# The first expert's blocks written out part by part on every engine, with the bounds check moved to the second expert

## The chip, the cores and the metric

The kernel runs on one core of one Trainium2 chip. A core has TensorE (PE, matrix products, with a queue of its own for loading weights), VectorE (DVE), ScalarE (ACT), GpSimd (POOL) and SyncE (SP, which only issues transfers here). Each engine runs its instructions in its own order; one that waits for a semaphore holds up all behind it on that engine. 16 DMA engines move data between HBM and SBUF. Products go to eight PSUM banks of 128 x 512 float32; the kernel uses five of them under the tag `big` and three under `att`.

The metric is the device time of one execution in microseconds. A run's time is a median of several executions.

## The reference

A linear attention with a decaying state, then two feed-forward layers ("experts"), all in float32. Four batches, eight heads of 48, 768 steps; 3072 tokens of width 384 in the two layers.

```python
# r, k, v: (4, 8, 768, 48), 0.1 * randn;  w the same shape, 0.8 to 0.95;  u: (8, 48)
state = zeros(B, H, D, D)
for t in range(S):
    kt, vt, rt, wt = k[:, :, t], v[:, :, t], r[:, :, t], w[:, :, t]
    cur = einsum('bhd,bhe->bhde', u[None] * kt, vt)
    y[:, :, t] = einsum('bhd,bhde->bhe', rt, state + cur)
    state = wt[..., None] * state + einsum('bhd,bhe->bhde', kt, vt)
x = y.transpose(0, 2, 1, 3).reshape(3072, 384)

a = x @ w1; b = x @ w2          # 384 -> 1024 each
x = ((a * b) @ w3) @ w_out      # 1024 -> 1024 -> 384
h = x @ w_in                    # 384 -> 2048
out = (h - tanh(h)) @ w_out2    # 2048 -> 384
```

The first layer's w1, w2, w3, w_out and the second layer's w_in, w_out arrive in float64.

## The kernel before

**Attention in chunks.** The 768 steps of a batch are six chunks of 128, 24 chunks (n) in all. `prep(n)` loads five tiles (P, ws: the decays twice; k, r, v), checks that the decays lie within bounds (two ScalarE passes, L210 and L211, into `over`), and forms the running product of the decays (a scan on VectorE, L214), its inverse from the end of each block of 8 (L217 on GpSimd, L218, and the scan L221 on VectorE) and the decayed k and r (L238, L239; on VectorE for the first four chunks, on GpSimd later). `att(n)` forms the scores (`psA`, L259, copied by L263 and masked on GpSimd, L265), turns k (`psk`, L278), updates the state (`psu`, L285) and adds up the outputs (`psy`, L301 and L307). The diagonal, r u k, is made by small matmuls and a product (L243, L295, L313) for n < 5, and by GpSimd products, a reduction and a predicated copy (L235 to L237, L270) later. The last two heads of a chunk go to a tile `y` and are spread by six small transfers per block (L326) to the rows of `xt` that the other heads leave free.

**Weights.** Each float64 weight block is loaded as pairs of 32-bit words (`st`, three buffers) and made float32 by two ScalarE passes (L142, L145) and two VectorE passes (L146, L148). Weights and activations are kept as a rounded part and a rest (`fp32r`, two halves), and `three` (L166 to L168) forms each product of 512 columns by three matmuls.

**The first expert** works on six blocks of 512 tokens (four chunks each). For each of eight slices f of the 1024 columns, `phase1` forms a and b (18 matmuls; `psa`, `psb`), ScalarE copies a (L375), VectorE multiplies (L376), and ScalarE and VectorE split the product into `g` (L362, L363). `phase2` multiplies g by W = w3 w_out (9 matmuls into three banks `acc`). W is not loaded: `fold(f)` makes it, slice by slice, from w3 and w_out (8 products of 384 columns in float32, `psW`, L340) during the first block and the beginning of the second. phase2 follows phase1 two or three slices later. `store` writes the block to HBM (`x2d`).

**The second expert** works on the same six blocks in sixteen slices (`phase3`, `psh`), with three ScalarE squares and three VectorE products per slice in place of the tanh, and w45 as weights. `decide` gathers the checks (bounds of the decays, sizes of the weights and of x) into one flag; if it is set, a slow general path runs at the end. It does not run on these inputs.

**Order.** Program order is that of the loops from L503 on: chunk 0 to 3 and three conversions, then in block 0 and 1 lists of further parts hung on the slices (`extra`, `before`). From this a scheduler with a model of the engines sets the order on each engine; it may move any instruction past others that it does not depend on.

Of the kernel before, what the change touches and what calls it, by code (L numbers as in the profile page):

```python
# [10 lines left out]
F32 = mybir.dt.float32  # L11
# [22 lines left out]
LAG = 3  # L34
SLOTS = 14
GB = 2
GP = LAG + 2
XL = 4
ATT = 0, 1, 2, 5
ATT0 = 2, 3, 5, 6  # L40
PED = 5
KD = 4

# [31 lines left out]
def body(ctx: ExitStack, tc, rT, kT, wP, wS, vN, rN, kN, vT, uB, uN, uP, w12, w3F, wo, w45, out):  # L75
# [21 lines left out]
    ends = [const.tile([128, NP, C // SB, SB], F32, name=f"ends{i}") for i in range(2)]  # L97
    for t in ends:
        nc.gpsimd.memset(t, 0.0)
# [27 lines left out]

    def words(src, n, dst=None, clamp=False):
# [4 lines left out]
        hw = st[:, :, 1]  # L133
        m = cvp.tile([128, n], I32, tag="cm", name="cm")

        if clamp:
            nc.scalar.activation(out=m.bitcast(F32), in_=hw.bitcast(F32), func=AF.Abs, scale=2.0**-112)
            nc.vector.tensor_scalar(out=m.bitcast(F32), in0=m.bitcast(F32), scalar1=TOP, scalar2=None, op0=ALU.min)
        else:
            i = len(used)  # L140
            used.append(i)
            nc.scalar.activation(out=m.bitcast(F32), in_=hw.bitcast(F32), func=AF.Abs, scale=2.0**-112, accum_out=tops[:, i : i + 1])  # L142

        l = cvp.tile([128, n], I32, tag="cl", name="cl", bufs=2)
        nc.scalar.activation(out=l, in_=fl(st).bitcast(U8)[:, 3::8], func=AF.Identity, scale=1 / 32, bias=qa[:, 5:6])  # L145
        nc.vector.scalar_tensor_tensor(out=m, in0=m, scalar=3, in1=l, op0=ALU.logical_shift_left, op1=ALU.bitwise_or)  # L146
        to = m if dst is None else dst.bitcast(I32)
        nc.vector.scalar_tensor_tensor(out=to, in0=hw, scalar=SIGN, in1=m, op0=ALU.bitwise_and, op1=ALU.bitwise_or)  # L148
        return to.bitcast(F32)
# [6 lines left out]
    def halves_of(src, name, vec=True, clamp=False):  # L156

        t = wtile(name)
        x = words(src, 2 * DM, clamp=clamp)
        nc.scalar.copy(t[:, 0, :], x)  # L160
        (nc.vector if vec else nc.gpsimd).tensor_sub(t[:, 1, :], x, t[:, 0, :].bitcast(F32))
        return t
# [24 lines left out]

    def xtile(blk):
# [6 lines left out]
    def prep(n):  # L195
        r_d = a2.tile([128, NP, C], F32, tag="rd", name="rd")
        k_d = a2.tile([128, NP, C], F32, tag="kd", name="kd")
        P = a2.tile([128, NP, C + 1], F32, tag="P", name="P")
        w_s = a2.tile([128, NP, C], F32, tag="ws", name="ws")
        v_n = a2.tile([128, H, 64], F32, tag="vn", name="vn")  # L200
        nc.sync.dma_start(P, wP[n])
        nc.sync.dma_start(w_s, wS[n])
        nc.sync.dma_start(k_d, kT[n])
        nc.sync.dma_start(r_d, rT[n])
        nc.sync.dma_start(v_n, vN[n])
        if n == 0:
            nc.sync.dma_start(fl(ub), uB)
# [7 lines left out]
        e = ends[n % 2]  # L215
        R = a1.tile([128, NP, C // SB], F32, tag="R", name="R")
        nc.gpsimd.tensor_scalar(out=R, in0=P[:, :, SB::SB], scalar1=3e38, scalar2=1e-25, op0=ALU.min, op1=ALU.max)  # L217
        nc.vector.reciprocal(e[:, :, :, SB - 1], R)  # L218
        sx = fl(w_s)
        back = e.rearrange("p a j s -> p (a j s)")[:, ::-1]  # L220
# [3 lines left out]
        cd = a2.tile([128, H], F32, tag="cd", name="cd")  # L224
        if n < PED:
            rk = a1.tile([128, NP, C], F32, tag="rk", name="rk")
            by.tensor_mul(rk, r_d, k_d)
        else:
            r_n = a1.tile([128, DM], F32, tag="rk", name="rn")
            k_n = a1.tile([128, DM], F32, tag="vc", name="kn")  # L230
            if n == PED:
                nc.sync.dma_start(un, uN.to_broadcast([128, DM]))
            nc.sync.dma_start(r_n, rN[n])
            nc.sync.dma_start(k_n, kN[n])
            nc.gpsimd.tensor_mul(r_n, r_n, un)  # L235
            nc.gpsimd.tensor_mul(r_n, r_n, k_n)
            nc.vector.tensor_reduce(out=cd, in_=r_n.rearrange("p (h d) -> p h d", d=D), op=ALU.add, axis=AX.X)  # L237
        by.tensor_mul(fl(k_d), fl(k_d), sx)  # L238
        by.tensor_mul(r_d, r_d, P[:, :, 0:C])  # L239
        if n < PED:  # L240
            pd = attp.tile([128, NP, 2], F32, tag="att", name="psd")
            for p in range(NP):
                nc.tensor.matmul(pd[:, p, :], rk[:, p, :], ub[:, p, :], start=True, stop=True)  # L243
# [476 lines left out]
```

## Time and profile before

| | |
|---|---|
| median of 3 runs | 955.73 us (954.77 to 956.27) |
| the profiled execution | 952.14 us, its span 950.4 us |
| TensorE busy | 876.2 us (92% of the span), mean granted clock 0.966 of full |
| VectorE, ScalarE, GpSimd busy | 623.2, 490.7, 223.7 us (66, 52, 24%) |
| stores of the first expert's blocks 3 and 4 | begin at 435.78 and 501.52 us |
| stores of the second expert's block 0, then each 65 us | 625.87, 691.14, 756.42 us |

The span is from the first to the last instruction. Busy shares are means over stages with different limits, so stretches of time say more than these. The granted clock is that of TensorE, as a share of 2.4 GHz; 0.5 is the lower level, 1.2 GHz. Matmuls overlap: a single one shows 0.39 us though the next starts 0.23 us after it.

### The profile page before, as it was taken

The numbers are of one execution on the slowest core, as the hardware profiler recorded it, in microseconds if no ns is written. First come the engines' busy times: TensorE is split into PE (matmuls) and PEld (weight loads), VectorE is DVE, ScalarE is ACT, GpSimd is POOL, SyncE is SP. The second block draws the span as 40 slices with busy tenths as digits, with TensorE's granted clock in tenths as the row PEclk, the third lists the DMA queues.
The fourth block names the chain that finished last, engine by engine and source line by source line (L and its number), as shares of the span: only waits on it lengthen the run. The fifth ranks groups of instructions, "written<-read, shape, count | busy, mean of one in ns | idle before, by whom it ended". The sixth has DMA issues, their size and how long they took to land.

```text
span 950.4 us, 12862 instructions
## 1 busy us (share of the span) xinstructions
PE 876.2 (92%) x4762; PEld 700.4 (74%) x4762; DVE 623.2 (66%) x885; ACT 490.7 (52%) x880; POOL 223.7 (24%) x217
## 2 busy tenths in 40 slices
PE   3556988889999999999999999999999999999996
PEld 3445765566877777777777778888888888888885
DVE  7970755657747557647457797676676666676763
ACT  5851444345433334333247676666666666666662
POOL 3231334332534434334224530010010010100000
PEclk9656999989999999999999999999999999999999
DMA  8853254455633343342034310010020110200001
GB/s 300 279 190 95 80 182 158 136 169 205 203 92 104 94 140 128 113 108 92 31 83 155 112 56 11 1 67 1 1 67 0 37 32 1 67 1 0 34 1 37
DMA packets 38951, 87.02 MB, mean 92 GB/s; under 512 B 4832, under 2 KB 9824, under 8 KB 38880
## 3 DMA queue, kind: packets, MB, share of 16 engines
q1 hardware_dynamic: 37152, 83.76, 26.6%
q10 hardware_dynamic: 1728, 2.36, 1.3%
q8 instruction: 39, 0.64, 0.3%
q14 instruction: 32, 0.26, 0.1%
HBM read 74.31 MB, written 9.44 MB: 88 GB/s over the span
## 4 chain that ended last, share of the span: by engine, by line
PE 61%; DMA 10%; DVE 9%; issue 8%; POOL 5%; ACT 4%; SPq 0%; POOLq 0%; ACTq 0%; DVEq 0%
PE acc L168 9%; PE acc L166 8%; PE acc L167 8%; PE psh L166 7%; PE psh L167 7%; PE psh L168 7%; DMA st<-w 3%; DMA st<-w3F 2%; DMA rn<-rN 2%; PE psb L166 2%; PE psa L166 2%; PE psA L259 2%; PE psb L167 1%; PE psy L307 1%; DVE A L270 1%
## 5 line engine op out<-in xcount | busy, mean ns | idle before, releaser
L363 DVE TENSOR_TENSOR g<-psh,g 128x512 fp32r<-128x512 f32 (+1 forms) x99 | 66.6, 674 | 61.2 <-ACT g L362 61.0
L166 PE MATMUL psh<-xt,w 128*128 128x512 f32 x252 | 98.1, 389 | 1.0 <-DVE g L363 1.0
L362 ACT CAST g<-psh 128x512 fp32r<-128x512 f32 (+1 forms) x99 | 56.7, 574 | 81.7 <-DVE psh L422 81.7
L167 PE MATMUL psh<-xt,w 128*128 128x512 f32 x252 | 98.0, 389 | 0.0
L166 PE MATMUL acc<-g,w 128*128 128x512 f32 x252 | 98.0, 389 | 0.0
L168 PE MATMUL psh<-xt,w 128*128 128x512 f32 x252 | 98.0, 389 | 0.0
L167 PE MATMUL acc<-g,w 128*128 128x512 f32 x252 | 98.0, 389 | 0.0
L168 PE MATMUL acc<-g,w 128*128 128x512 f32 x252 | 98.0, 389 | 0.0
L420 DVE TENSOR_TENSOR psh<-psh,z 128x512 f32<-128x512 f32 (+1 forms) x99 | 67.3, 680 | 28.1 <-ACT z L417 28.0
L359 POOL TENSOR_TENSOR xt<-x2l,xt 128x512 fp32r<-128x512 f32 x18 | 24.5, 1375 | 252.6 <-ACT xt L358 252.5
L417 ACT ACTIVATE z<-psh 128x512 f32<-128x512 f32 (+1 forms) x99 | 58.0, 586 | 41.4 <-PE psh L168 39.8
L362 ACT CAST g<-psb 128x512 fp32r<-128x512 f32 x48 | 28.1, 585 | 97.2 <-DVE psb L376 84.5
L146 DVE SCALAR_TENSOR_TENSOR cm<-cm,cl 128x768 int32<-128x768 int32 (+1 forms) x44 | 44.9, 1021 | 45.2 <-ACT cl L145 37.7
L422 DVE SCALAR_TENSOR_TENSOR psh<-s,psh 128x512 f32<-128x512 f32 (+1 forms) x99 | 67.2, 679 | 10.2 <-DVE psh L421 0.9
L421 DVE SCALAR_TENSOR_TENSOR psh<-s,psh 128x512 f32<-128x512 f32 (+1 forms) x99 | 67.1, 678 | 8.5
L418 ACT ACTIVATE s<-z,qa 128x512 f32<-128x512 f32 (+1 forms) x99 | 70.6, 713 | 3.0
L166 PE MATMUL psa<-xt,w 128*128 128x512 f32 x144 | 59.8, 415 | 12.9 <-DMA xt<-y 11.3
L419 ACT ACTIVATE s<-z,qa 128x512 f32<-128x512 f32 (+1 forms) x99 | 68.9, 696 | 0.0
L142 ACT ACTIVATE cm<-st 128x768 f32<-128x768 f32 (+1 forms) x44 | 36.2, 823 | 51.5 <-DMA st<-w3F 34.7
L166 PE MATMUL psb<-xt,w 128*128 128x512 f32 x144 | 59.2, 411 | 3.0 <-ACT a L375 2.5
L168 PE MATMUL acc<-g,W 128*128 128x512 f32 x144 | 54.3, 393 | 3.9 <-DVE W L363 3.9
L166 PE MATMUL acc<-g,W 128*128 128x512 f32 x144 | 56.6, 393 | 1.1 <-ACT W L362 1.1
(132 smaller groups left out, 2017.9 us busy)
## 6 DMA issues: line engine op xcount, KB each, us to landing
st<-w SPq DMA_DIRECT2D x24, 768.0 KB, 4.4
st<-w3F SPq DMA_DIRECT2D x16, 512.0 KB, 4.5
P<-wP SPq DMA_DIRECT2D x24, 258.0 KB, 3.0
ws<-wS SPq DMA_DIRECT2D x24, 256.0 KB, 2.7
kd<-kT SPq DMA_DIRECT2D x24, 256.0 KB, 3.1
rd<-rT SPq DMA_DIRECT2D x24, 256.0 KB, 3.9
vn<-vN SPq DMA_DIRECT2D x24, 256.0 KB, 3.6
x2d<-o SPq DMA_DIRECT2D x18, 256.0 KB, 2.2
```

The source lines that it names most:

```text
L146: nc.vector.scalar_tensor_tensor(out=m, in0=m, scalar=3, in1=l, op0=ALU.logical_shift_left, op1=ALU.bitwise_or)
L166: nc.tensor.matmul(ps, lhs(0), rhs(1), start=start, stop=False)
L167: nc.tensor.matmul(ps, lhs(0), rhs(0), start=False, stop=False)
L168: nc.tensor.matmul(ps, lhs(1), rhs(0), start=False, stop=stop)
L362: nc.scalar.copy(t[:, 0, :], x)
L363: nc.vector.tensor_sub(t[:, 1, :], x, t[:, 0, :].bitcast(F32))
L417: nc.scalar.activation(out=z, in_=p, func=AF.Square)
L418: nc.scalar.activation(out=s1, in_=z, func=AF.Square, scale=QS, bias=qa[:, 0:1])
L419: nc.scalar.activation(out=s2, in_=z, func=AF.Square, scale=QS, bias=qa[:, 1:2])
L420: nc.vector.tensor_mul(p, p, z)
L421: nc.vector.scalar_tensor_tensor(out=p, in0=s1, scalar=QB1, in1=p, op0=ALU.add, op1=ALU.mult)
L422: nc.vector.scalar_tensor_tensor(out=p, in0=s2, scalar=QB2, in1=p, op0=ALU.add, op1=ALU.mult)
```

## The change

The first five blocks of the first expert are no longer ordered by the scheduler.

*Block 0 and the first eight chunks* are split into parts that each use one engine (`running`, `scores`, `mask`, `w_scaled`, `s_round` and so on), and a table `ORDER` of some 400 words, read from left to right, says which part of which chunk, weight block or slice comes next. A word is a short name and a number: `Sa3` the scores of chunk 3, `lwa3`, `waa3`, `wba3`, `wja3`, `wha3`, `wsa3` the load, the two ScalarE passes, the VectorE passes, the rounding and the rest of block 3 of w1 and w2 (`a`; `o` is w_out, `x` and `y` the halves of w3), `P3` and `Q3` phase1 and phase2 of slice 3, `F3` fold 3. All of chunks 0 to 7 and all eight folds come before the end of block 0.

*Blocks 1 to 4* follow a function `pair`: one chunk of the next block and two slices of this one, in a fixed order.

*The first four chunks' last two heads* are not sent through transfers: their outputs come first in `psy`, are copied (`last_out`), and three matmuls with a tile of ones and zeros (`last_place`) add them to the free rows of the same bank. For later blocks the six transfers are issued by SyncE, not ScalarE.

*The bounds check* reads the decays again during the second expert's blocks 1 to 4 (six chunks each, `bounds`), and `decide` runs in block 5 instead of block 1. The diagonal by small matmuls is used for n < 4 (was 5), the two `ends` tiles are one, and w3 has four buffers (were three). Block 5 of the first expert and the second expert are still ordered by the scheduler.

```diff
-PED = 5
+PED = 4
+ORDER = """
+LP0 LK0 lwa3 lwa1 lwa2 Da0 LP1 Dr0 K0 Db0 LK1 Dk0 Sd0 Dc0 waa3 wba3 Sa0 Se0 wja3 waa1 Sf0 wba1 St0 lwy3 Sb0 wja1 Sk0
...
+""".split()
-        d2 = ev.tile([128, NP, C], F32, tag="a", name="d2")
-        nc.scalar.activation(out=d2, in_=P[:, :, 1:], func=AF.Square, bias=qa[:, 2:3])
-        nc.scalar.activation(out=d2, in_=d2, func=AF.Relu, bias=qa[:, 4:5], accum_out=over[:, n : n + 1])
...
+        order = (KT, *range(KT)) if blk == 0 else range(NP)
+        for p in order if c else ():
...
+    def last_out(n):
+        nc.scalar.copy(last2()[1], preps[n]["py"][:, KT, :])
+
+    def last_place(n):
+        sel, y = last2()
+        for j in range(KT):
+            nc.tensor.matmul(preps[n]["py"][:, j, :], sel[:, j, :], y, start=False, stop=True, skip_group_check=True)
...
+    w3_tile = lambda: cvp.tile([128, NF // 2, 128], F32, tag="w3", name="w3", bufs=4)
...
+    with tc.manual_schedule():
+        nc.sync.dma_start(fl(ub), uB)
+        for x in ORDER:
+            k = x.rstrip("0123456789")
+            parts[k](int(x[len(k) :]))
+        store(acc0, lambda e: x2d[0, :, e, :], 0)
...
+    def pair(blk, i, acc, weights):
+        n = (blk + 1) * per + i
...
+        f = 2 * i
+        if now:
+            scores(n)
+            scores_out(n, 0)
+            mask(n, 0)
+            scores_out(n, 1)
+            mask(n, 1)
+            turn = n % NC < NC - 1
+            if turn:
+                turned(n)
+                turned_out(n)
+        pa, pb = phase1(xtile(blk), f)
+        a = gate_a(pa)
+        if nn:
+            load2(n + 2, "ws")
+            load2(n + 2, "k")
+        if now:
+            put_diag(n)
+        nc.vector.tensor_mul(pb, pb, a)
+        g = gp.tile([128, 2, TB], F32R, tag="g", name="g")
+        split_ps(pb, g)
+        if weights and i == 3:
+            conv2_halves(blk - 2)
+            largest(blk - 2)
+        if now and turn:
+            update(n)
+            state(n)
+            state_decay(n)
+        done(f, g)
+        if nn:
+            load2(n + 2, "P")
+        if nx:
+            running(n + 1)
+            block_ends(n + 1)
+            backward(n + 1)
+            decayed(n + 1)
+            ruk(n + 1)
+        if now:
+            outputs(n)
+        if weights and i == 1:
+            conv2_fetch()
+        f += 1
+        pa, pb = phase1(xtile(blk), f)
+        if now:
+            for part in (last_round, last_rest, x_round, x_rest):
+                part(n)
+            if i == per - 1:
+                spread(blk + 1, nc.sync)
+        if nn:
+            load2(n + 2, "r")
+            load2(n + 2, "v")
+        if nx:
+            ruk_sum(n + 1)
+        if nn:
+            load_n(n + 2, "kn")
+            load_n(n + 2, "rn")
+        a = gate_a(pa)
+        nc.vector.tensor_mul(pb, pb, a)
+        g = gp.tile([128, 2, TB], F32R, tag="g", name="g")
+        split_ps(pb, g)
+        if weights and i == 2:
+            conv2_act(blk - 2)
+            conv2_join(blk - 2)
+        done(f, g)
+
+    for blk in range(1, NB - 1):
+        acc = []
+        with tc.manual_schedule():
+            for i in range(per):
+                pair(blk, i, acc, blk in (2, 3))
...
+    def bounds(n):
+        w = ev.tile([128, NP, C], F32, tag="a", name="wb")
+        nc.sync.dma_start(w, wP[n][:, :, 1:])
+        nc.scalar.activation(out=w, in_=w, func=AF.Square, bias=qa[:, 2:3])
+        nc.scalar.activation(out=w, in_=w, func=AF.Relu, bias=qa[:, 4:5], accum_out=over[:, n : n + 1])
...
-        if blk == 1:
-            extra[2].append(decide)
+        if 0 < blk < NB - 1:
+            for j in range(6):
+                extra[2 * j + 2].append(lambda n=6 * blk - 6 + j: bounds(n))
+        if blk == NB - 1:
+            extra[2].append(decide)
```

How the instructions stand on an engine, before and now, at three places.

The first place is ScalarE around the copies of chunk 3's scores (`A<-psA`). `cm` and `cl` are the two passes of a weight conversion (128x768 a block of w1 and w2 or w_out, 128x512 a half of w3), `xt` and `y` the outputs of chunk 2 and then 3, `ks` the turned k. Before:

```order
L142 ACTIVATE cm,tops<-st 128x768
L145 ACTIVATE cl<-st,qa 128x768
L142 ACTIVATE cm,tops<-st 128x512
L145 ACTIVATE cl<-st,qa 128x512
L320 CAST xt<-psy 128x3x128
L320 CAST y_246<-psy 128x128
L145 ACTIVATE cl<-st,qa 128x512
L263 COPY A<-psA 128x512 x2
L280 COPY ks<-psk 128x512
```

Now:

```order
L168 ACTIVATE cm,tops<-st 128x768
L312 COPY cd<-psd 128x8
L430 CAST xt<-psy 128x3x128
L332 COPY A<-psA 128x512 x2
L174 ACTIVATE cl<-st,qa 128x768
L354 COPY ks<-psk 128x512
L168 ACTIVATE cm,tops<-st 128x768
L409 COPY y_148<-psy 128x128
```

The copies stood behind two whole conversions and the second pass of another half of w3 (128x512). Now they follow chunk 2's outputs directly, with one pass of a conversion of w_out ahead of those and the other behind the copies.

The second place is TensorE where block 1's first product (`psa<-xt` with block 0 of the weights) begins; `psW` is a fold, `acc` the second layer's product, `psA` and `psk` scores and turned k of chunk 8. Before:

```order
L301 MATMUL psy<-rd,Sb_120 64x128 x8
L307 MATMUL psy<-A,vn 64x128 x8
L340 MATMUL psW<-wo,w_1106 128x384 x4
L340 MATMUL psW<-wo,w_1107 128x384 x4
L259 MATMUL psA<-rd,kd 128x128 x8
L278 MATMUL psk<-ident,kd 128x128 x4
L166 MATMUL psa<-xt,w_0_182 128x512
L167 MATMUL psa<-xt,w_0_182 128x512
```

Now:

```order
L327 MATMUL psA<-rd,kd 128x128 x2
L486 MATMUL psW<-wo,w_1166 128x384 x4
L486 MATMUL psW<-wo,w_1362 128x384 x4
L327 MATMUL psA<-rd,kd 128x128
L486 MATMUL psW<-wo,w_1366 128x384 x4
L486 MATMUL psW<-wo,w_1248 128x384 x4
L327 MATMUL psA<-rd,kd 128x128 x2
L206 MATMUL acc<-g,W 128x512
...
L208 MATMUL acc<-g,W 128x512
L327 MATMUL psA<-rd,kd 128x128 x3
L349 MATMUL psk<-ident,kd 128x128 x4
L206 MATMUL psa<-xt,w_0_442 128x512
```

Chunk 7's outputs (`psy`) stood one fold, the scores and the turned k ahead of block 1's first product. Now they stand further up, and two folds and the second layer's products stand between.

The third place is VectorE during one pair of slices of blocks 1 to 4; `psb<-psb,a` is the gate product, `g` its rest, `P` and `ws` the two scans of the next chunk, `A<-eye,cd` the diagonal, `cd<-rn` the reduction that feeds the next chunk's diagonal. Before:

```order
L214 SCALAR_TENSOR_TENSOR P<-P,e_86 128x516
L218 RECIPROCAL ends_89<-R 128x64
L221 SCALAR_TENSOR_TENSOR ws<-ws,ends_89 128x512
L376 TENSOR_TENSOR psb<-psb,a 128x512
L270 COPY_PREDICATED A<-eye,cd 128x512
L363 TENSOR_TENSOR g<-psb,g 128x512
L270 COPY_PREDICATED A<-eye,cd 128x512
L237 TENSOR_REDUCE cd<-rn 128x8
L291 TENSOR_TENSOR Sb_119<-psu,Sb_120 128x4x48
L321 TENSOR_TENSOR xt<-psy,xt 128x3x128
L321 TENSOR_TENSOR y_2186<-psy,y_2186 128x128
L376 TENSOR_TENSOR psb<-psb,a 128x512
```

Now:

```order
L343 COPY_PREDICATED A<-eye,cd 128x512 x2
L804 TENSOR_TENSOR psb<-psb,a 128x512
L516 TENSOR_TENSOR g<-psb,g 128x512
L370 TENSOR_TENSOR Sb_117<-psu,Sb_118 128x4x48
L261 SCALAR_TENSOR_TENSOR P<-P,e_86 128x516
L289 RECIPROCAL ends<-R 128x64
L292 SCALAR_TENSOR_TENSOR ws<-ws,ends 128x512
L426 TENSOR_TENSOR y_2203<-psy,y_2203 128x128
L434 TENSOR_TENSOR xt<-psy,xt 128x3x128
L285 TENSOR_REDUCE cd<-rn 128x8
L843 TENSOR_TENSOR psb<-psb,a 128x512
L516 TENSOR_TENSOR g<-psb,g 128x512
```

The reduction, which waits for two products on GpSimd, stood behind the diagonals and between two gate products that are far apart; now it stands just ahead of each pair's second gate product, and the two scans stand between the pair's two gate products.

## Rows read from the trace of the kernel before

**Rows 1.** Stretches of the span: start:end, length, then by engine busy us (instructions), granted clock, DMA.

```profile
10.00:60.00 50.00, 29.49 (x222) 25.89 (x224) 47.36 (x59) 35.99 (x69) 15.22 (x13) 0.73 0.78 274
30.00:60.00 30.00, 17.06 (x127) 14.78 (x128) 28.36 (x38) 21.49 (x42) 8.90 (x8) 0.56 0.73 242
60.00:90.00 30.00, 15.35 (x141) 13.25 (x138) 7.12 (x10) 8.24 (x18) 7.41 (x8) 0.61 0.46 139
90.00:200.00 110.00, 94.57 (x549) 67.92 (x548) 64.62 (x86) 45.96 (x97) 38.68 (x38) 0.96 0.42 133
200.00:240.00 40.00, 39.65 (x242) 27.20 (x240) 25.31 (x34) 18.16 (x34) 15.18 (x15) 1.00 0.55 198
240.00:280.00 40.00, 40.00 (x248) 31.77 (x245) 25.86 (x35) 15.51 (x30) 17.04 (x16) 1.00 0.45 145
560.00:950.40 390.40, 382.61 (x1689) 316.19 (x1687) 266.70 (x408) 242.36 (x403) 21.05 (x16) 1.00 0.08 25
```

**Rows 2.** Chain of waits at the front: start us, us, what.

```profile
0.82 2.75 DMA P<-wP
...
4.93 0.73 ACT d L210
...
5.68 1.25 DVE P L214
```

**Rows 3.** The same chain further on.

```profile
69.65 3.87 DMA st<-w3F
...
74.26 1.05 ACT A L263 x2
...
187.38 6.54 DMA xt<-y
```

**Rows 4.** TensorE's timeline: start, length, operation, idle before and its releaser.

```profile
37.56 1.97 PE L301 MATMUL psy<-rd,Sb 48*64 48x128 f32 x16
...
88.03 0.77 PE L166 MATMUL psa<-xt,w 128*128 128x512 f32 x1 [5.30 <-DMA xt<-y]
...
91.38 0.39 PE L168 MATMUL psa<-xt,w 128*128 128x512 f32 x1
...
105.66 0.39 PE L168 MATMUL psb<-xt,w 128*128 128x512 f32 x1
```

**Rows 5.** Chain of waits: one fold, and one chunk's TensorE work at full clock.

```profile
202.37 5.36 PE psW L340 x16
...
239.08 1.09 PE psA L259 x16
...
240.17 0.59 PE psk L278 x4
...
246.45 0.60 PE psu L285 x16
...
247.06 1.02 PE psy L301 x16
...
248.08 1.02 PE psy L307 x16
```

**Rows 6.** VectorE's timeline: the product rk twice.

```profile
7.80 0.63 DVE L227 TENSOR_TENSOR rk<-rd,kd 128x512 f32<-128x512 f32 x1
...
11.80 1.47 DVE L227 TENSOR_TENSOR rk<-rd,kd 128x512 f32<-128x512 f32 x1
```

**Rows 7.** GpSimd's timeline beside it.

```profile
10.64 2.08 POOL L295 TENSOR_TENSOR vc<-vn,cd 128x512 f32<-128x512 f32 x1 [3.34 <-ACT cd L244]
```

**Rows 8.** SyncE's timeline: the stores of the first expert's blocks 3 and 4.

```profile
435.78 3.36 SPq L397 DMA_DIRECT2D x2d<-o  x3
...
501.52 4.12 SPq L397 DMA_DIRECT2D x2d<-o  x3
```

**Rows 9.** Groups of ScalarE instructions, 0 to 200 us: count, busy us, mean ns, idle before.

```profile
L210 ACT ACTIVATE d<-P,qa 128x512 f32<-128x512 f32 x10 | 7.1, 721 | 3.1 <-DMA P<-wP 3.0
L211 ACT ACTIVATE d<-d,qa 128x512 f32<-128x512 f32 x9 | 6.5, 721 | 0.2
```

More of the change, by code (lines that the diff above doesn't have):

```diff
@@ L256, in att, with diag_out, diag_v, scores @@
+    def diag_out(n):
+        nc.scalar.copy(preps[n]["cd"], fl(preps[n]["pd"]))
+    def diag_v(n):
+        t = preps[n]
+        t["vc"] = a1.tile([128, H, 64], F32, tag="vc", name="vc")
+        nc.gpsimd.tensor_mul(t["vc"], t["v"], t["cd"].unsqueeze(2).to_broadcast([128, H, 64]))
+    def scores(n):
+        t = preps[n]
+        r_d, k_d = t["r"], t["k"]
+        t["pss"] = [attp.tile([128, NP, C], F32, tag="att", name="psA") for _ in range(2)]
+        t["A"] = [None] * 2
         for p in range(NP):
@@ L293, in att, with scores_out @@
[L293 to L298 removed]
+                nc.tensor.matmul(t["pss"][q][:, p, :], k_d[o : o + D, p, :], r_d[o : o + D, p, :], start=True, stop=True)
+    def scores_out(n, q):
+        t = preps[n]
+        t["A"][q] = a2.tile([128, NP, C], F32, tag=f"A{q}", name="A")
+        nc.scalar.copy(t["A"][q], t["pss"][q])
@@ new lines, in turned_out, with update, state @@
+    def turned_out(n):
+        t = preps[n]
+        t["ks"] = a2.tile([128, NP, 128], F32, tag="ks", name="ks", bufs=1)
+        nc.scalar.copy(t["ks"], t["pk"])
+    def update(n):
+        t = preps[n]
+        t["pu"] = attp.tile([128, NP, D], F32, tag="att", name="psu")
+        for h in range(H):
+            p, q = divmod(h, 2)
+            o = 64 * q
+            nc.tensor.matmul(t["pu"][o : o + 64, p, :], t["ks"][:, p, o : o + 64], t["v"][:, h, :D], start=True, stop=True)
+    def state(n):
+        t = preps[n]
+        dst = Sb[(n + 1) % 2][:, :, :D]
+        if n % NC == 0:
+            nc.vector.tensor_mul(dst, t["pu"], t["P"][:, :, C : C + 1].to_broadcast([128, NP, D]))
+        else:
+            nc.vector.tensor_add(dst, t["pu"], Sb[n % 2][:, :, :D])
@@ new lines, in x_rest, with spread, prep @@
+    def x_rest(n):
+        py, x, _ = place(n)
+        nc.vector.tensor_sub(x[:, 1], py[:, :KT, :], x[:, 0].bitcast(F32))
+    def spread(blk, queue):
+        xt, y3 = xtile(blk), y3tile(blk)
+        for q in range(2):
+            for j in range(KT):
+                a, b = 64 * q + 16 * j, 64 * q + D
+                queue.dma_start(xt[b : b + 16, :, j, :].bitcast(F32), y3[a : a + 16].bitcast(F32))
+    def prep(n):
+        load(n, 0)
+        load(n, 1)
+        running(n)
+        block_ends(n)
+        load_rk(n)
+        ruk(n)
+        ruk_sum(n)
+        backward(n)
+        decayed(n)
@@ L329, in body, with att @@
+    def att(n):
+        if n not in preps:
+            prep(n)
+        scores(n)
+        for q in range(2):
+            scores_out(n, q)
+            mask(n, q)
+        put_diag(n)
+        if n % NC < NC - 1:
+            for part in (turned, turned_out, update, state, state_decay):
+                part(n)
+        for part in (outputs, last_round, last_rest, x_round, x_rest):
+            part(n)
+        if (n + 1) * C % TB == 0:
+            spread(n * C // TB, nc.scalar)
     w12t, Wt, w45t = [None] * NF, [None] * NF, [None] * NF2
+    w3_half = lambda f, i: (w3F[f][:, i * 512 : (i + 1) * 512], 512)
@@ L639, in body @@
         wot.clear()
[L640 to L642 removed]
+        for m in range(NF // 2):
+            words(wo[m], 2 * DM, wo_half(m), True)
+        wpair.clear()
         for f in range(NF):
```

460 lines of the change are left out of this document (270 added, 190 removed).

## The prediction

> **What bounds the kernel now.** I read the table of stretches first [rows 1]. Look along its PE column: later TensorE is busy 98 to 100% of the time (40.00 of 40 us from 240 on, 382.61 of 390.4 from 560 on), so there only less TensorE work, or fewer gaps, could help. Before 200 us it is not: 15.35 of 30 us from 60 to 90, 94.57 of 110 from 90 to 200. Most of what can be gained lies in the first 200 us. In 10 to 60 us the DVE column is full (47.36 of 50), but from 60 to 90 it falls to 7.12 of 30: the engine that bounded the start has stopped, and so has everything else.
>
> The chain of waits says why. At the front, the first scan on VectorE starts at 5.68 although its data landed at 3.57: ScalarE's bounds check on the same tile stands between [rows 2]. Later, the copy of chunk 3's scores starts at 74.26 behind a conversion that waits for a w3 load issued only at 69.65 [rows 3]; ScalarE runs in order, so the attention chain waits for weights that only the later folds need. And from 187.38 on block 1's products wait through 6.54 us of small transfers into xt [rows 3]; block 0's first one starts at 88.03 after the same kind of wait, 5.30 us [rows 4].
>
> **The change, part by part.** I count to one point that both kernels pass: the first store of block 4's result, at 501.52 [rows 8]. After it the instructions are the same apart from the bounds check.
>
> *1. Up to the first product.* VectorE has 55 instructions between its first scan and the last piece of chunk 3 (rows 10 to 64 of its written order). At the mean of 10 to 60 us, 47.36/59 = 0.80 us [rows 1], that is 44 us; at the same 95% share of busy time, 47 us. With the bounds check gone the first scan can start at 3.6 [rows 2], so VectorE alone would allow the first product at 50. TensorE is the other bound. A chunk takes 1.09 + 0.59 + 0.60 + 1.02 + 1.02 = 4.3 us at 2.4 GHz [rows 5]; the diagonal's matmuls, as many as L307's, add 1.0, and 0.7 is an estimate for the eight small ones and the three that place rows: 6 us. At 1.2 GHz it is twice that: L301 took 1.97 us at 37.56 against 1.02 [rows 4, 5], and the granted clock was 0.56 and 0.61 of full speed in 30 to 90 us [rows 1]. Four chunks are then 47 us (chunk 0 has no state product), from about 8 us: 55, and with 2 us a chunk for the copy and the mask between scores and outputs 63. So the first product starts between 50 and 63. I take 60, near the slow end, because TensorE will again wait between short bursts as it did when rows 1 showed the low level. Before: 88.03.
>
> *2. From there to the end of block 0.* The TensorE work is fixed. The products of both layers are 8 x 27 = 216 matmuls at 0.2267 us (63 steps between 91.38 and 105.66 [rows 4]) = 49.0; eight folds at 5.36 [rows 5] = 42.9; chunks 4 to 7 are 4 x 4.32, less chunk 4's scores (done before), chunk 5's two state steps and chunk 6's state product (1.09 + 1.19 + 1.02) = 14.0. Sum 106 us. The waits inside: bounded below by 0.35 of 40 us (200 to 240) and above by 15.4 of 110 (90 to 200) [rows 1]. Of the 15.4, 6 were the wait for the small transfers at 187.38 [rows 3], which now have two folds and 18 matmuls, 15 us, between their issue and their use; the other 9.4 of 110, 8.5%, I keep: 9 us. Bounds 1 to 15. Block 0 ends at 60 + 106 + 9 = 175.
>
> *3. Blocks 1 to 4.* Their work does not change: 900 matmuls of the products (four blocks and block 5's first two steps) x 0.2267 = 204.0, and sixteen chunks x 4.32 less five missing steps (2 x 1.02 + 3 x 1.19) = 63.5; sum 267.5. The method checks against the two stores: 49.0 + 4 x 4.32 - 1.0 = 65.3 for a block, measured 501.52 - 435.78 = 65.7 [rows 8]; so I add 2 for four blocks, and 1.5 from the last matmul to the store. What changes is who waits. In the new order VectorE's second gate product stands behind the reduction L285, which waits for two GpSimd products, and those wait for the backward scan. Behind that gate product are the copy and the subtraction that free the PSUM bank which TensorE needs one step later. From 240 to 280 VectorE and GpSimd worked 25.86 and 17.04 of 40 us [rows 1]: beside a step pair of 16.3 us that is 10.5 and 6.9. If they never overlapped, 17.5 us, each of the 16 pairs would lose 1.2: 19 us. The other wait that comes late is the transfers into xt, now on SyncE: 6.54 us from issue to use [rows 3] with only one second-layer step (9 x 0.2267 = 2.0), the scores and the transpose (1.7) and a little scalar work in front: 2 us at each of four block ends, 8 us. I take 8; bounds 0 and 19.
>
> *4. The bounds check.* 24 x (0.72 + 0.72) = 35 us of ScalarE [rows 9] move into the second expert's blocks 1 to 4, with 24 loads of 256 KB on SyncE's queue, which also holds the outputs and the loads of x2. Behind a check that waits for its load are ScalarE's squares, and VectorE waits for these. In 560 to 950 ScalarE was busy 242.36 of 390.4 and TensorE 382.61 [rows 1]: 148 us idle on ScalarE hide it, and five products are ahead of their use. I take 0; without that cover it would be up to 35.
>
> The three-to-four buffer change of w3 and the move of the decision to block 5 I cost at nothing: they stand beside TensorE at 98%, and a wait there would show as a gap of it.
>
> *The sum.* Block 4's store at 175 + 267.5 + 2 + 1.5 + 8 = 454 against 501.5: 47.5 us earlier. The profiled execution took 952.14 (span 950.4), so 904.6 for one like it; the runs' median is 955.73, 3.6 above that execution, and the same difference gives **908 us**.
>
> **A page of the Trainium skill that speaks against it.** The product rk took 0.63 us at 7.80 and 1.47 at 11.80 [rows 6], when GpSimd's vc ran from 10.64 to 12.72 [rows 7]. The Trainium skill, SBUF — State Buffer, section "SBUF: two separate sides", says that VectorE instructions with two SBUF inputs and GpSimd instructions share one port pair, and that the one which starts second is blocked for the whole of the other. These rows agree. By that rule GpSimd's 22 instructions before the first product (13 in 10 to 60 us of the old kernel, 1.17 us each) would hold VectorE some 10 us longer (an estimate), and its bound for the first product would be 60, not 50; the forecast would stay, and the first rival below would lose its chance.
>
> **The rivals.**
> *The order runs as tightly as its sums.* TensorE gets its full clock early and VectorE bounds the start: first product at 52, 1 us of waits after it, 3 in blocks 1 to 4. Block 0 ends at 159; 21 us less: 887. For it: VectorE's 95% share in 10 to 60. Against: the granted clock of 0.56 to 0.61.
> *TensorE stays slow and the engines wait for one another.* First product at 66, 15 us of waits, 12 in blocks 1 to 4: 924. For it: the clock rows, and that a fixed order puts one late load in front of all that is behind it.
> *The order does not do what it says.* VectorE has 155 instructions up to the end of block 0, 124 us at 0.80; at its share of 10 to 200 us, 47.36 + 7.12 + 64.62 of 190 [rows 1], that is 198 us, and the last two folds (10.7) come behind its last conversions: 209, 34 more than I count: 942, and with the products behind the folds up to 956. For it: three weight buffers, one of them held long by a half of w3's block 3. Against: the idle of 60 to 90 us had one cause, which the order takes away.
> *Slower: the pairs of blocks 1 to 4 are too tight.* One mechanism: TensorE waits in each pair for the PSUM bank behind gate product, reduction, GpSimd and scan. With VectorE, GpSimd and ScalarE strictly in turn, 25.86 + 17.04 + 15.51 of 40 us [rows 1], a pair takes 23.8, not 16.3. It decides from 47.5/16 = 3.0 us a pair; at 4 us it costs 64 in place of my 8: 964. Against: each engine's own work is well under 16.3, and most of the three overlap.
>
> **How the numbers follow.** Forecast 0.57 (its own range, from the first product at 55 to 63, waits of 5 to 13, and 3 to 14 in the blocks: 894 to 921), tight 0.14, slow clock 0.17, no gain from the order 0.05, slower 0.07. About 0.2%, 2 us, is what a measurement here can tell from no change. Of the 0.05 I put 0.03 on faster and 0.02 on the same. Faster 0.57 + 0.14 + 0.17 + 0.03 = 0.91, same 0.02, slower 0.07. The range 892 to 932 holds the forecast, all but the slow edge of the slow clock, and the near part of the tight case, some 0.8.
>
> **What the new profile would show.** Right: the first psa matmul near 60; the first scan at about 3.6; no stretch before 175 in which VectorE is idle for 10 us; no wait of psa for xt<-y of more than 2 us; block 4's x2d store near 454; the last 450 us as before. Step 1 is wrong if the first product starts before 52 or after 66; step 2 if TensorE's idle between it and block 0's last matmul is over 15 us; step 3 if TensorE waits in blocks 1 to 4 sum to over 19; step 4 if a wait of TensorE or VectorE there ends on the load of w. The whole is wrong if the granted clock or a queue makes block 0 end after 200.

## The result, and the profile after

The changed kernel takes **909.48 us** (median of 4 runs, 908.82 to 910.88); the kernel before, on the same chip, 955.25 (954.17 to 956.27). The ratio is 0.9523, with a 95% interval of 0.9506 to 0.9539. The profiled execution took 908.82 us, its span 907.1, against 952.14 and 950.4.

The same stretches as in [rows 1], from the changed kernel (length, then the busy time of each engine with its count, the granted clock, the DMA share and GB/s):

```profile
10.00:60.00 50.00, 38.16 (x387) 33.01 (x386) 43.36 (x50) 29.52 (x57) 21.62 (x21) 0.83 0.70 232
30.00:60.00 30.00, 22.42 (x264) 19.55 (x260) 26.85 (x32) 14.76 (x30) 13.95 (x13) 0.82 0.70 224
60.00:90.00 30.00, 28.38 (x159) 21.79 (x160) 25.69 (x31) 16.08 (x32) 18.38 (x16) 0.94 0.73 244
90.00:200.00 110.00, 106.72 (x617) 76.34 (x616) 69.59 (x101) 42.05 (x89) 30.45 (x31) 1.00 0.46 145
560.00:907.10 347.10, 339.64 (x1499) 280.60 (x1497) 230.91 (x356) 239.02 (x424) 15.38 (x12) 1.00 0.14 41
```

The hole is gone: from 60 to 90 TensorE is busy 28.38 us, not 15.35, and VectorE 25.69, not 7.12; from 90 to 200 TensorE has 106.72 of 110. The last stretch is full in both kernels.

TensorE's first product, which answers to [rows 4], and on SyncE the stores of blocks 0 to 4, which answer to [rows 8]:

```profile
60.02 0.50 PE L206 MATMUL psa<-xt,w 128*128 128x512 f32 x1 [1.56 <-DVE xt L434]
```

```profile
175.03 2.12 SPq L557 DMA_DIRECT2D x2d<-o  x3
256.25 2.12 SPq L557 DMA_DIRECT2D x2d<-o  x3
326.18 2.12 SPq L557 DMA_DIRECT2D x2d<-o  x3
401.62 2.12 SPq L557 DMA_DIRECT2D x2d<-o  x3
460.38 0.82 SPq L557 DMA_DIRECT2D x2d<-o  x2
```

The first product came 28.0 us earlier, block 4's store 41.1 (501.52 before). From that store to the end of the span there were 448.9 us before, and 446.7 now. So 41 of the 43 us were won up to block 4's store. From block 1's store to block 4's it takes 204.1 us, which is no less than before (203.7, from 297.80 to 501.52): all of the gain lies in front of it. In that stretch TensorE has less to do than before (busy 194.8 us, not 200.8), since more was done ahead of it, and is idle longer (9.4 us, not 3.0).

What TensorE waited for, from the first product to block 0's store and from there to block 4's (us in total, times, longest):

```profile
PE acc L208 <- DVE W L202: 2.2, 1, 2.2
PE psA L327 <- POOL kd L303: 1.6, 1, 1.6
PE psa L206 <- DVE xt L434: 1.6, 1, 1.6
```

```profile
PE psA L327 <- POOL kd L303: 3.5, 2, 2.5
PE psa L206 <- DMA xt<-y: 3.3, 1, 3.3
PE psa L206 <- ACT A L332: 1.9, 1, 1.9
PE psu L362 <- ACT ks L354: 1.6, 2, 1.4
```

### The profile page after: what moved, and what is told of

It is laid out like the page before. It is cut to its first block, busy times and chain, and to the rows that moved or that the text cites. A ratio compares the mean times of both kernels' runs of the same rounds, so it can differ in the third digit from the quotient of the medians.

```text
span 907.1 us, 12892 instructions
## 1 busy us (share of the span) xinstructions
PE 861.9 (95%) x4762; PEld 690.8 (76%) x4762; DVE 614.3 (68%) x884; ACT 483.0 (53%) x879; POOL 227.3 (25%) x223
## 4 chain that ended last, share of the span: by engine, by line
PE 49%; issue 3%; POOL 2%; DVE 1%; DMA 1%; ACT 1%; SPq 0%; ACTq 0%; POOLq 0%
PE acc L206 8%; PE acc L208 8%; PE acc L207 8%; PE psh L206 7%; PE psh L208 7%; PE psh L207 7%; POOL w L202 1%; DMA st<-w 1%; PE psa L206 1%; PE psa L207 1%; PE psa L208 1%; PE psb L207 1%; PE psb L206 1%; PE psb L208 1%; PE psy L395 0%
## 5 line engine op out<-in xcount | busy, mean ns | idle before, releaser
L515 ACT CAST g<-psb 128x512 fp32r<-128x512 f32 x40 | 23.4, 585 | 84.9 <-DVE psb L843 48.8
L206 PE MATMUL psa<-xt,w 128*128 128x512 f32 x144 | 61.8, 429 | 6.9 <-DMA xt<-y 3.3
L337 POOL TENSOR_SCALAR_AFFINE_SELECT A<-A 128x512 f32<-128x512 f32 x48 | 37.6, 804 | 90.9 <-ACT A L332 90.7
L206 PE MATMUL psb<-xt,w 128*128 128x512 f32 x144 | 56.9, 395 | 2.5 <-ACT a L531 2.2
L208 PE MATMUL acc<-g,W 128*128 128x512 f32 x144 | 56.3, 391 | 2.2 <-DVE W L202 2.2
L206 PE MATMUL acc<-g,W 128*128 128x512 f32 x144 | 57.8, 401 | 0.0
L207 PE MATMUL psa<-xt,w 128*128 128x512 f32 x144 | 57.6, 400 | 0.0
```

The costliest lines, as they stand in the source:

```text
L206: nc.tensor.matmul(ps, lhs(0), rhs(1), start=start, stop=False)
L207: nc.tensor.matmul(ps, lhs(0), rhs(0), start=False, stop=False)
L208: nc.tensor.matmul(ps, lhs(1), rhs(0), start=False, stop=stop)
L337: nc.gpsimd.affine_select(out=A, in_=A, pattern=[[0, NP], [1, C]], compare_op=ALU.is_gt, fill=0.0, base=0, channel_multiplier=-1)
```

## The experiments

Each was timed in five rounds beside the kernel before on the same chip, and its ratio is to those runs. Four chips were used, so ratios compare better than microseconds do; the changed kernel's are 0.9523 above and 0.9527 below. Its second run, on the same chip as the kernels with sixteen extra matmuls, without block 5's conversions in block 3, and with both edits, is the measure unless another is named.

**The changed kernel again.** 

> The changed kernel once more, so that the next three have it on their own chip: 907 to 914, first product at 60, block 0's store at 175, block 3's interval of 75 us.

Measured: 908.49 us (907.52 to 911.75), ratio 0.9527 (0.9498 to 0.9557). First product 59.96, block 0's store 174.10, block 3's interval 75.0.

**Block 0's order left to the scheduler.**

```
-    with tc.manual_schedule():
+    with nullcontext():
         nc.sync.dma_start(fl(ub), uB)
         for x in ORDER:
```

> Block 0's parts are written in the same order, but the scheduler may place them as it likes; the rest is the changed kernel. Theory A (it is the order that is worth the time, not that the work is cut into parts): the scheduler again puts late weight loads and their conversions ahead of the attention chain, the first product with w_12 starts at 75 to 90 instead of 60.0, and the time is 925 to 945. Theory B (cutting the work into parts of one engine each, and placing the last heads by matmul, is what helps): first product at 58 to 66, time 906 to 916.

Measured: 947.84 us, ratio 0.9930 (0.9906 to 0.9953); first product 92.92, block 0's store 212.65, 37.6 us late. ScalarE's and TensorE's waits in that kernel, 45 and 40 to 93 us:

```profile
ACT cm L168 <- DMA st<-w3F: 6.4, 3, 2.9
ACT y L409 <- PE psy L401: 5.9, 1, 5.9
```

```profile
PE psu L362 <- ACT ks L354: 6.4, 2, 4.0
PE psy L414 <- ACT y L409: 5.9, 1, 5.9
```

As in [rows 3], ScalarE stands in front of conversions that wait for w3, and TensorE for the copies behind them. Theory A holds, and 948 is past its range: the same parts, without the order, keep 7 of the 46 us. This kernel has the fourth w3 buffer as well, so that buffer by itself does not end the wait for w3. How much of the 38 us is the w3 load, and how much the rest of the order, is not separated.

**The pairs' order left to the scheduler.**

```
     for blk in range(1, NB - 1):
-        with tc.manual_schedule():
+        with nullcontext():
             for i in range(per):
                 pair(blk, i, acc, blk in (2, 3))
```

> The pairs of blocks 1 to 4 are written in the same order, but the scheduler may place them; block 0 stays in its written order. Theory A (the written order of the pairs is worth nothing by itself: 204.1 us from block 1's store to block 4's against 204.3 in the kernel before): within 4 us of the changed kernel, 905 to 914. Theory B (the pairs' order gives back the four waits for the transfers into xt, and it is only hidden by the 7 us lost in block 3): 915 to 925, with waits of 5 us of psa for xt<-y at the block ends.

Measured: 916.04 us, ratio 0.9587 (0.9552 to 0.9622), 6 to 7.5 us more than the changed kernel. Neither theory fits: the time is in B's range, but psa waits for xt<-y only once, 2.9 us. Block 0's store comes at 181.51, 6.5 us late, though block 0's order was kept; from there to block 4's (468.04) it takes 286.5 us, against 285.4 and 286.8 with the order. The stores hide that work has moved: before block 0's store TensorE did fifteen more products of block 1 (81 each for psa and psb, not 75 and 72; 3.4 us), and the second stretch has that many fewer and still takes as long. So block 0 lost some 4 us behind its first product, and the pairs' order, against A, is worth some 3 to 5 us in blocks 1 to 4. In block 0 TensorE waits once for ScalarE; ScalarE's rows just before show why:

```profile
168.40 0.50 PE L206 MATMUL acc<-g,W 128*128 128x512 f32 x1 [3.95 <-ACT W L199]
```

```profile
163.00 0.98 ACT L174 ACTIVATE cl<-st,qa 128x768 int32<-128x768 uint8 x1
167.00 0.98 ACT L174 ACTIVATE cl<-st,qa 128x768 int32<-128x768 uint8 x1 [3.02 <-DMA st<-w]
167.88 0.47 ACT L199 CAST W<-psW 128x384 fp32r<-128x384 f32 x1
```

These 128x768 conversions are of the second expert's w45; the check of its size (L657), which follows each, stands there at 170.61. Eight loads of w were issued between 135 and 181 us, none in the changed kernel. With the pairs freed, the scheduler put them inside block 0, and the fold's copy stood behind one that waited for its load. A written order keeps its own instructions in sequence; it doesn't keep others out.

**The bounds check back ahead of each scan.**

```
+        d2 = ev.tile([128, NP, C], F32, tag="a", name="d2")
+        nc.scalar.activation(out=d2, in_=P[:, :, 1:], func=AF.Square, bias=qa[:, 2:3])
+        nc.scalar.activation(out=d2, in_=d2, func=AF.Relu, bias=qa[:, 4:5], accum_out=over[:, n : n + 1])
```

> The bounds check goes back ahead of each forward scan (two ScalarE instructions of 0.72 us a chunk, 24 chunks), and the second expert has none. Theory A (only the first scan feels it, 2.1 us, and the pairs hide the rest): first scan at 5.7, first product at 61 to 64, time 911 to 914. Theory B (in a fixed order ScalarE's 1.44 us stand in front of the scan of every pair): 1 us or more for each of 16 pairs on top, 922 to 935.

Measured: 918.63 us, ratio 0.9617 (0.9583 to 0.9652), 9 to 10 us more. First product 62.59, block 0's store 182.04, block 4's 469.82. Of the 7 us at block 0's store 2.6 are there at the first product and 4.4 come later in block 0; blocks 1 to 4 lose 1 to 2.4. So A is right on the pairs (B's 1 us a pair is not there), and too low on block 0. From block 4's store to the end of the span there are 447.5 us without the check in the second expert and 446.7 with it: there it is free.

**The kernel before, with only the check moved.** 

> The kernel before, with its scheduler, and only the bounds check moved to the second expert's blocks 1 to 4 and the decision to block 5. Theory A (what the kernel with the check put back lost, 9 us, is the price of ScalarE's 1.44 us a chunk in front of each scan in any order): first product some 4 us before 88, time 944 to 949. Theory B (it costs that only where the order is fixed and the start is tight; in the kernel before the stall of 60 to 90 us, which waits for a w3 load, covers it): first product at 86 to 89, time 952 to 957.

Measured: 954.84 us against 954.49, ratio 1.0002 (0.998 to 1.0023). The first scan starts at 3.65 (5.68 before), the first product at 86.80. Theory B: with its scheduler and its stall the kernel before loses nothing by the check (the chain of waits still runs through a w3 load, 4.71 us at 61.28); in the written order the check costs 9 to 10. The two parts of the change don't add.

**Block 0's last heads by transfers.**

```
-        "V": lambda n: last_out(n) if n < per else last_round(n), "W": ... last_place(n) ..., "Z": lambda n: spread(1, nc.sync)
+        "V": last_round, "W": last_rest, "Z": lambda n: spread(n // per, nc.sync)
```

> In block 0 the last two heads are again moved into xt by twelve SyncE transfers after chunk 3, in place of the three matmuls and copies of each chunk that place them. Theory A (the transfers were on the path in block 0: 5.30 us of waiting at 88.03 in the kernel before): first product 3 to 6 us later, 63 to 66, time 912 to 916. Theory B (another chain ends at the same time, so they are hidden): first product within 1 us of 60, time 908 to 911.

Measured: 918.26 us, ratio 0.9617 (0.9583 to 0.9651). TensorE:

```profile
70.73 0.77 PE L206 MATMUL psa<-xt,w 128*128 128x512 f32 x1 [11.27 <-DMA xt<-y]
```

Theory A, and more: 10.7 us at the first product, 8.7 left at block 0's store. TensorE waited 11.27 us for the six transfers (six, not the twelve of the text above); before it had been 5.30 [rows 4].

**Sixteen matmuls ahead of the first one.**

```
+        wm0 = big.tile([128, TB], F32, tag="big", name="wm0")
+        for _ in range(WARM):   # 16
+            nc.tensor.matmul(wm0[:, :128], ident, ident, start=True, stop=True)
```

> Sixteen 128x128 matmuls of the identity, whose result nobody uses, stand ahead of the first psd matmul on TensorE; the rest is the changed kernel. Theory A (TensorE at its lower level up to 34 us sets the first product): TensorE gets its full clock earlier, the first product starts at 52 to 57, the time is 902 to 906. Theory B (VectorE, with GpSimd beside it, sets it, and TensorE's clock is hidden): first product at 59 to 61, the time within 2 us of the changed kernel; if the extra matmuls delay the first psd, up to 3 us later.

Measured: 909.63 us, ratio 0.9527 (0.9496 to 0.9558); first product 61.49. TensorE's first work in the changed kernel (first run), then in this one:

```profile
8.58 1.87 PE L309 MATMUL psd<-ub,rk 128*128 128x2 f32 x8 [8.58 <-DVE rk L297]
10.38 2.08 PE L327 MATMUL psA<-rd,kd 48*128 48x128 f32 x16
...
24.14 2.50 PE L327 MATMUL psA<-rd,kd 48*128 48x128 f32 x16 [1.06 <-issue]
...
36.28 1.16 PE L327 MATMUL psA<-rd,kd 48*128 48x128 f32 x16
```

```profile
2.20 6.70 PE L750 MATMUL wm<-ident 128*128 128x128 f32 x32 [2.20 <-POOL ident masks.py:199]
9.23 1.05 PE L310 MATMUL psd<-ub,rk 128*128 128x2 f32 x8 [0.33 <-DVE rk L298]
10.56 1.16 PE L328 MATMUL psA<-rd,kd 48*128 48x128 f32 x16 [0.28 <-DVE kd L304]
```

The sixteen (counted as 32 there) brought the full clock to these two groups: the scores took 1.16 us, as they do at 36.28, and not 2.08. It did not last. The next matmuls on TensorE, psk, waited 2.53 us for ScalarE and took 1.12 (0.66 at full clock, at 37.51 in the changed kernel), and chunk 1's scores took 2.49, as without the sixteen. So nearly all of the lower level before 34 us was still there, and theory A was not tested. Nor are the 1.5 us at the first product shown to come from the clock: ScalarE's first weight conversion, ahead of the copy that psk waits for, began at 10.99 and not 9.19, when its load had landed; and with the same sixteen and one more edit (below) the first product came at 60.19. An estimate of what is left for theory A: at 36.90 VectorE had waited 2.65 us for chunk 1's outputs, and behind that it hardly waited; a full clock up to there would win 2.65 us at most by this wait.

The row of stretches must not be read for this: it gives the changed kernel a granted clock of 1.00 from 10 to 20 us, where the scores took 2.08 us.

**wo's conversions behind the end of xt.**

```
-... Db4 lwo3 wao2 wjo1 Dc4 ... T3 X3 lwa4 wjo2 wao3 U3 Sa4 LP5 wbo3 Y3 lwy0 P0 Sb4 wjo3
+... Db4 lwo3 wao2 Dc4 ... T3 X3 U3 Sa4 LP5 Y3 P0 wjo1 lwa4 wao3 wjo2 wbo3 lwy0 Sb4 wjo3
```

> In block 0's written order the conversions of wo's blocks 1 and 2 move behind the subtraction that completes xt; with them the later loads that need their buffers. The rest is the changed kernel. In its trace VectorE is idle for 0.2 us from 36.9 to 60.0, and these four instructions, at 53.96, 54.92, 57.33 and 58.54, take 5.0. Theory A (VectorE's queue sets the first product): it starts at 55 to 56.5; if nothing behind it is short of VectorE, the time is 4 to 5 us less than the changed kernel, 903 to 906; if TensorE then waits for the folds of wo instead, the gain is given back by block 0's store. Theory B (TensorE's lower level sets it): first product at 59 to 61, time 907 to 911.

Measured: 910.77 us, ratio 0.9525 (0.9499 to 0.9551); first product 59.10, 0.9 earlier for 5.0 us less on VectorE. The end of chunk 3 on TensorE in this kernel:

```profile
51.35 1.12 PE L349 MATMUL psk<-ident,kd 128*128 128x128 f32 x4 [3.40 <-DVE xt L434]
52.40 1.97 PE L389 MATMUL psy<-rd,Sb 48*64 48x128 f32 x16
...
57.00 0.94 PE L414 MATMUL psy<-y 128*128 128x128 f32 x6
57.87 1.16 PE L327 MATMUL psA<-rd,kd 48*128 48x128 f32 x16
59.10 0.50 PE L206 MATMUL psa<-xt,w 128*128 128x512 f32 x1
```

Without the two conversions VectorE waits for TensorE (2.34 and 1.05 us before L370 and L434), and the first product follows straight on chunk 4's scores. The numbers are theory B's. The rows say more than B: TensorE's chain ends last, but it waited 3.40 us for VectorE on the way, and its lower level here (psy in 1.97 us, not 1.09) came behind that wait. The two engines' chains end within 1 us of each other.

**All of wo's conversions there.** 

> The same with all of wo's conversions, on ScalarE too: block 0's 2.6 us at 45.90 and block 3's besides, and the later loads that need their buffers come later still. Theory A: first product at 52 to 54; the conversions that are put off then meet the gates and the chunks 4 and 5 on VectorE, which was busy 25.7 of 30 us from 60 to 90, so at most half of the 7 us is left at block 0's store: 903 to 908. Theory B (TensorE's lower level): first product at 58 to 61, and 908 to 914.

Measured: 913.13 us, ratio 0.9551 (0.9527 to 0.9576). The first product is in neither theory's range; the time is in B's. First product 56.95, 3.0 earlier, because the 3.40 us in front of psk (VectorE's xt behind wo's first conversion) fell to 0.18. Block 0's store came at 176.53, later than the 174.10 and 175.03 of the changed kernel: the work put off is met again by chunk 4. TensorE, 60 to 100 us:

```profile
PE psy L395 <- DVE A L343: 3.6, 2, 3.4
PE psA L327 <- POOL kd L303: 2.0, 1, 2.0
```

An earlier first product was worth nothing by itself in this order.

**No conversion of block 5 inside block 3.** The changed kernel loses 7 us of TensorE between 346 and 386. VectorE's order there has four conversions (L178, L180). The pairs of block 3 ask for one; the other three belong to block 5 (the text below says four; with its edit one is left).

```
+    lq = const.tile([128, 2], F32, name="lq");  last = xtile(NB - 1)[:, 1, 0, TB - 1 : TB].bitcast(F32)
+    nc.scalar.activation(out=lq[:, 0:1], in_=last, func=AF.Identity, scale=0.0, bias=qa[:, 5:6])
...
-        ... func=AF.Identity, scale=1 / 32, bias=qa[:, 5:6])
+        ... func=AF.Identity, scale=1 / 32, bias=late[0][:, 0:1] if late else qa[:, 5:6])
```

> The conversions of w45 that belong to block 5 get a bias column that is computed from the last chunk's part of xt, so none of them can be placed inside block 3's pairs, where four stood. The rest is the changed kernel. Theory A (the four conversions hold VectorE, ScalarE and the backward scan there, and cost block 3 about 9 us of its 75.4 with the low clock behind them): block 3's interval falls to 65 to 68, up to 2 us come back in block 5, and the time is 900 to 904. Theory B (block 3's gap comes from GpSimd's products, which psA waited for 2.5 us): block 3 stays at 72 to 76 and the time within 2 us of the changed kernel.

Measured: 912.78 us, ratio 0.9556 (0.9524 to 0.9588). Three stretches of the changed kernel, then of this one:

```profile
326.00:400.00 74.00, 66.77 (x448) 52.64 (x446) 46.87 (x64) 27.72 (x51) 29.61 (x31) 0.95 0.56 182
400.00:460.00 60.00, 60.00 (x384) 48.10 (x382) 37.07 (x54) 22.61 (x42) 21.41 (x21) 1.00 0.25 77
460.00:560.00 100.00, 96.99 (x418) 79.16 (x417) 79.38 (x114) 69.83 (x118) 29.92 (x17) 0.98 0.25 82
```

```profile
326.00:400.00 74.00, 71.41 (x479) 56.49 (x478) 47.36 (x65) 21.27 (x43) 29.54 (x31) 0.98 0.49 159
400.00:460.00 60.00, 57.98 (x366) 46.07 (x365) 35.62 (x52) 25.05 (x48) 21.67 (x21) 0.99 0.26 82
460.00:560.00 100.00, 93.93 (x398) 76.46 (x397) 80.33 (x112) 72.08 (x120) 31.70 (x18) 0.96 0.30 99
```

The three conversions did cost block 3: its interval falls from 75.0 to 70.4, half of what A said. But 5 us of TensorE are lost from 400 to 560; from 460 on VectorE is busy 80 us of 100, and TensorE waits 6.0 us there for VectorE's g. The time is 4 us above the second run of the changed kernel, with intervals that overlap: that the three conversions were cheaper where the scheduler had put them is likely, and not shown.

**That edit and the sixteen matmuls.** 

> The last two edits together. If they add: the gain of the one and the gain of the other against the changed kernel within 1 us, from 895 (both theories A) to 910 (neither).

Measured: 911.00 us, ratio 0.9534 (0.9506 to 0.9563), between the two: nothing to add.

**The conversions let into block 4.** The same edit with `xtile(NB - 2)`. 

> As in the kernel that kept w45's conversions out of block 3, but the bias column is computed from block 4's xt, so that they may be placed in block 4, where TensorE was busy 59.0 of 59 us and VectorE 36. Theory A (they cost what they push aside where they are placed, and block 4 has room): block 3's interval 70 to 71 as there, block 4's 59 to 60, none of the 8 us lost in block 5: 903 to 906. Theory B (the conversions cost the same anywhere before the second expert): block 4's interval 62 to 65, 908 to 912.

Measured: 906.65 us (906.54 to 908.24), ratio 0.949 (0.9468 to 0.9511). Block 3's interval is 74.4, not 70 to 71, block 4's 58.3, and block 4's store comes at 458.85. So theory A's gain is not where it said. Part of it is there all the same: with the three conversions behind 380 us, TensorE no longer waits for GpSimd's kd and ScalarE's ks in block 3 (2.5 and 1.4 us), only for xt<-y (3.0), and block 4's first product comes at 377.28, not 381.63. Of these 4.4 us, 2.0 do not show in block 3's interval because nine more products of block 4 stand ahead of its store. At 2 to 3 us less than the changed kernel this is the fastest of all, but the intervals overlap: that it is faster is likely, and not shown.

## Why the prediction was right

*Step 1: right in number, and partly by luck.* The first product was put at 60, from TensorE at its lower level between 55 and 63, with VectorE alone at 50. It came at 60.02. But TensorE was not at its lower level all the way: chunk 1's scores took 2.50 us at 24.14, chunk 2's 1.16 at 36.28, and only from 50.65 on, behind a wait of 3.40 us for VectorE, did it run slowly again (granted clock 0.82 from 30 to 60). And VectorE set more of it than was forecast: it was busy 48.1 us with the 55 instructions, 0.87 each and not 0.80, from a first scan at 4.48 and not 3.6 (its data landed later). Without any wait that ends at 52.6, and from 36.9 to 60 it waited 0.2 us. The bound of 50 was too low, and the engines end together: a lighter VectorE moved the start by 0.9 and 3.0. What a full clock before 34 us would have moved is open.

Part of what VectorE took longer is GpSimd beside it. VectorE, then GpSimd, in the changed kernel:

```profile
48.49 1.65 DVE L261 TENSOR_TENSOR_SCAN P<-P,e 128x516 f32<-128x516 f32 x1
...
53.96 0.93 DVE L178 SCALAR_TENSOR_TENSOR cm<-cm,cl 128x768 int32<-128x768 int32 x1
54.92 1.91 DVE L180 SCALAR_TENSOR_TENSOR wo<-st,cm 128x768 int32<-128x768 int32 x1
```

```profile
47.99 2.58 POOL L337 TENSOR_SCALAR_AFFINE_SELECT A<-A 128x512 f32<-128x512 f32 x2 [0.24 <-ACT A L332]
...
54.11 1.90 POOL L303 TENSOR_TENSOR kd<-kd,ws 128x512 f32<-128x512 f32 x1 [1.16 <-DVE ws L292]
```

L180 takes 0.96 us at 58.54, when GpSimd is idle. The rule that the prediction weighed (the Trainium skill, SBUF — State Buffer, section "SBUF: two separate sides": the one that starts second is blocked for the whole of the other) fits this pair: L303 ended at 56.01, and 0.96 after that is 56.97; L180 ended at 56.83. The scan at 48.49, beside the two selects at 47.99, took 1.65 in place of 1.23. The first select alone took 1.07 us, to 49.06; by the rule the scan would have ended at 50.29, and it ended at 50.14, as near as the other pair. The second select does not fit: it began at 49.0, and by the rule it would have waited for the scan and ended 1.07 us behind it, at 51.2; it took 1.55 and ended at 50.57. There the trace doesn't bear out a full block. In all VectorE took 4 us longer than the sum said, where the prediction's estimate by the rule was 10.

*Step 2: the sum right, its terms not.* 175 was forecast, as 106 of work and 9 of waits; block 0's store began at 175.03. TensorE was busy 111.1 us from 60 to 175 and idle 3.9. A granted clock of 0.94 in 60 to 90 is 1.8 us of the 5 too many. Another 2.4 are chunk 8's scores and turned k and block 1's first three products (1.09 + 0.59 + 3 x 0.2267), which come ahead of the store and were not in the sum. Of the 9 us of waits, 8.5% carried over from the kernel before, 3.9 came; that the two errors cancel to 0.03 us is luck.

*Step 3: the mechanism partly, and 6.4 us too early.* Block 4's store was forecast at 454 and came at 460.38. From 175 to there TensorE was idle 10.5 us, where 8 were taken, and busy 274.9, where 271 were. Not the transfers at each of four block ends, but one place cost most, at the end of block 3; the chain of waits:

```profile
373.15 2.07 issue
375.24 1.27 POOL kd L303
376.53 0.33 SPq L772
376.95 0.59 SPq L441
...
378.86 2.63 DMA xt<-y
381.63 0.76 PE psa L206
382.40 0.43 PE psa L207
```

The wait for xt<-y is the predicted one, 3.3 us, more than the 2 that were named as a sign of being wrong; at the other three ends it did not show. Behind it the matmuls take 0.43 us each and not 0.23 (granted clock 0.66 from 376 to 386): the nine from 381.63 to 385.79 took 4.16 us and not 2.04. These 2.1 us are about half of the busy time that was not forecast; the rest is not traced. GpSimd's kd is late because the scan ws, which it waits for, stood behind the conversions of block 5 in VectorE's queue: in the last experiment, with them behind 380 us, this wait is gone and the one for xt<-y stays. No instruction of block 5 was counted in blocks 1 to 4; the written order was read for what it holds back, not for what is put into it. The pair chain through L285, for which up to 19 us were kept, did not appear among the waits.

*Step 4: right.* The 24 checks take 38.9 us of ScalarE (17.0, 17.3 and 4.6 for the reads of the sum, 0.19 each, which I had not counted) beside a TensorE that is busy 339.64 of 340 us from 560 to 900. No TensorE wait ends on their loads.

*After block 4's store* nothing was forecast; 2.2 us were won. 46 of the 47.7 us in the sum came, because step 3's shortfall of 6.4, these 2.2 and another 2.9 partly cancel: the runs stood nearer to the profiled execution (0.7 above it, not 3.6). That the time came within 1.5 us of the forecast is luck to this extent; the order of size of each step was right.

The rivals: the tight order (first product at 52) and the slow clock (at 66) are answered by 60.02; that the order doesn't do what it says by block 0's store at 175.03, not 209, and by the kernel without the order (948); the slower one, pairs that are too tight, by 285.4 us with the order against 286.5 without it and with less work.

## What to carry to other kernels

Look first at a stretch where all engines fall idle together, and follow the chain to the one queue that holds the wrong thing in front: here the written order of block 0, which takes the attention out from behind such loads, was worth 38 us, and three other parts of the change 6 to 10 each beside it. Alone, in the kernel before, the check's move was worth nothing; the others were not tried alone. Before you put a loss down to a stretch between two stores, count the matmuls in it: work may have moved across the store. When an order is written out, read it also for instructions from later code that the scheduler puts in between, and price them at every place to which they could go. An engine that is relieved of 5 us in front of a milestone says little, if the next chain ends 1 us later.

## What the runs showed of the hardware

- Sixteen extra matmuls from 2.2 to 8.9 us gave TensorE its full clock for the next two groups (1.05 and 1.16 us, in place of 1.87 and 2.08); behind a wait of 2.53 us it was at the lower level again (psk 1.12 us, not 0.66). The row of stretches gives a granted clock of 1.00 from 10 to 20 us for the kernel without them and 0.58 for the one with them: at the start of a span the durations of the matmuls are the safer reading.
- TensorE gaps of some 3 us were followed by matmuls at 1.2 GHz. Behind 3.40 us, from 47.2 to 50.7, a group of sixteen (L389) took 1.97 us in place of 1.09. Behind 3.33 us, before 381.63, nine matmuls took 4.16 us in place of 2.04: the wait cost 2.1 us more behind it. Without block 5's conversions the gap there was 2.59 us, and the first four matmuls still ran at full clock, the next eight not.
- The same six small transfers were waited for 11.27 us beside the weight loads of the start (issued from 61.49 to 67.7, directly behind a weight block and two tiles of a chunk), and 3.3 us in block 3 (issued from 376.95 to 380.7).
